# A depthwise convolution and a feed-forward block on one core: the fourth input load in one transfer, the last group but one added on VectorE, and the order of work in the first groups

## The chip, the core and the metric

The kernel runs on one core of a Trainium2 chip. The core has five engines that run side by side, each with its own queue of instructions: TensorE (PE, matmuls; its weight loads are listed as PEld), VectorE (DVE), ScalarE (ACT), GpSimd (POOL) and SyncE (SP), which here only issues transfers. Transfers (DMAs) run on 16 DMA engines and can be issued from several queues. Time is device microseconds (us) of one launch; lower is better. All times of instructions and transfers below are counted from the start of the span of the profiled execution.

## What is computed

The input x has 8 batches of 4224 positions and 192 channels. A causal convolution of 7 taps runs along the positions; the 192 channels are 8 heads of 24, and all channels of a head share the 7 weights, which are a softmax over the taps. On its result a feed-forward block with a normalisation in front and a residual is applied, with 768 hidden units.

```python
# convolution: w is a softmax over K=7 taps for each of H=8 heads
x_pad = np.concatenate([np.zeros((B, K - 1, D)), x], axis=1)
x_unf = x_pad[:, idx, :].reshape(B, S, K, H, group)
y = np.einsum('hk,bskhg->bshg', w, x_unf).reshape(B, S, D)
# feed-forward block
mu, var = mean and variance of y over D
xn = (y - mu) / np.sqrt(var + 1e-06) * g_ln
out = y + np.maximum(xn @ w_ch1, 0.0) @ w_ch2
```

All of it is float32. The first six positions of every batch see zeros on their left: this is the pad.

## The kernel before

**Groups.** The 33,792 positions are cut into 18 groups (lines 70 to 74). A position lies on one of 128 partitions, and a group holds up to 16 positions of each partition. Group 0 is the first 6 of batch 0, group 1 the 8 positions a partition that are left over from all batches (`LEFT`), group 2 the second 16 of batch 0; then come batches 1 to 7 in two groups each (3 to 16); group 17 is the 10 positions of batch 0 that group 0 left out. Groups 0 and 1 share their buffers (y, yt, ot).

**What a group goes through.** `load_x` brings x of the group, with 6 positions to the left, into a buffer `xg` (two buffers take turns; x3 takes the one of x1, so its load waits until the taps of group 1 are done). Tap products: `first_tap` (line 366) writes tap 0 to `y` on ACT at line 375, `second_tap` (385) and for group 2 `third_tap` write taps 1 and 2 to other buffers at line 383, and `add_in_parts` (402) adds these to y or to one another by four adding transfers that POOL issues at line 406. The other taps are added by `conv` (408) on DVE at line 414. `transpose` (425) makes yt, DVE's `moments` (445) and POOL's `root` (447) make the reciprocal root of the variance, `rstd`. The mean and g_ln are folded into w_ch1, so rstd is needed only at the very end. The up-projection fills sets of four PSUM banks, two sets in turn, and ACT evicts them with the ReLU. The down-projection follows, and `out = y + rstd * ot` ends the group.

**Groups 0 and 1** use a plain form: `up` (541), one chunk of 128 hidden units (f = 0 to 5) after the other, eviction on ACT at line 510, then `down` (809, matmuls at line 807). Between the chunks other ACT work is put by hand. For group 0 that is the tap products of group 1, w1's last copies (`copies_of_w1`, line 357) and `scale_power` (243), a part of decoding the weights. For group 1 it is `between` (534): the tap products of group 3, beginning behind chunk 2's eviction.

**Groups 2 to 17** use a form with seven products in place of eight, in `up_mixed` (600) or, for the last group, `up_last` (728), and in `down_fast` (841). It needs sums and differences of quarters of y and of the weights: `sums_of_y` (582), `sums_of_quarters` (569). Products are closed by DVE at line 640 or 750, or by adding transfers at line 598. A product's matmuls are at line 520 (up) and 860 (down).

**How a group ends.** For all groups but the last, y is stored to `out` by `store_y` (483) from SP. Later ACT scales ot by rstd (`scale`, 943) and POOL issues transfers that add ot to `out` in memory (`add_to_out`, 954). For group 16 this later work stands in `up_last`, except that DVE scales the first four positions (768). The last group adds on DVE (`add`, 956) and stores from SP (`store`, 963).

**The order** of all instructions of an engine is the order in which the program writes them (`manual_schedule`): each engine works through its own queue and stands until what an instruction needs is there. In the pass of the main loop for group 0 (1031 to 1056) stand: `conv` of group 1 in parts, the tap products of group 2, `store_y(1)` (eight stores), `load_x(3)`, moments, `down(0)`, the first part of `root(0)`, the adds of group 2's third tap (1053), the rest of `root(0)` and a difference of w1's quarters.

**The load of x3** is the one that the change touches. With `apart`, `load_x` clears the pad (one partition, 6 positions; line 163, on POOL) and then issues three transfers: partitions 16 to 127, 1 to 15, and partition 0 without the pad. The loads of other first halves of a batch (line 155) are one transfer, with the pad cleared behind it (161).

**The start.** Before w1 is decoded, `keep_warm` (359) issues matmuls whose result nobody reads. One `keep_warm` unit shows as two matmul records of line 362.

Of the kernel before, what the change touches and what calls it, by code (L numbers as in the profile page):

```python
# [11 lines left out]
ALU = mybir.AluOpType  # L12
# [4 lines left out]
def kernel(  # L17
# [29 lines left out]
    nc = tc.nc  # L47
    PSUM = bass.MemoryType.PSUM
    B, S, D = x.shape
    H, K = weight.shape  # L50
    F = moe_w_ch1.shape[1]
    P = 128
# [75 lines left out]

    xg = {}

    def load_x(g, queue=nc.sync, apart=False, gate=False):
        b, j0, n = groups[g]
        t = xpool.tile([P, J + PAD, D], F32, tag="xg", name=f"xg{g}")
        xg[g] = t
        flat = t.rearrange("p j d -> p (j d)")
        if gate:
            nc.vector.memset(t[0 : 1 if b is not None else P, 0:1, 0:1], 0.0)
        if b is None:
            for b in range(B):
                (queue if b < B // 2 else nc.gpsimd).dma_start(  # L140
                    out=flat[LP * b : LP * b + LP, 0 : (PAD + n) * D],
                    in_=bass.AP(
                        tensor=x.tensor, offset=(b * S + P * R - PAD) * D,
                        ap=[[n * D, LP], [1, (PAD + n) * D]],
                    ),
                )
            return
        if j0:
            queue.dma_start(
                out=flat[:, 0 : (n + PAD) * D], in_=xr[b, :, (j0 - PAD) * D : (j0 + n) * D]  # L150
            )
            return
        if b and not apart:

            queue.dma_start(
                out=flat[:, 0 : (PAD + n) * D],
                in_=bass.AP(
                    tensor=x.tensor, offset=(b * S - PAD) * D, ap=[[R * D, P], [1, (PAD + n) * D]]
                ),
            )  # L160
            nc.gpsimd.memset(t[0:1, 0:PAD, :], 0.0)
            return
        nc.gpsimd.memset(t[0:1, 0:PAD, :], 0.0)
        for p0, p1 in ((16, P), (1, 16)):
            nc.sync.dma_start(
                out=flat[p0:p1, 0 : (PAD + n) * D],
                in_=bass.AP(
                    tensor=x.tensor, offset=(b * S + p0 * R - PAD) * D,
                    ap=[[R * D, p1 - p0], [1, (PAD + n) * D]],
                ),  # L170
            )
        nc.sync.dma_start(out=flat[0:1, PAD * D : (PAD + n) * D], in_=xr[b, 0:1, 0 : n * D])
# [69 lines left out]
    def scale_power(power):  # L242
        nc.scalar.activation(power, power, AF.Relu, scale=float(1 << 23), bias=low)
# [297 lines left out]
    def up(g):  # L541


        n = groups[g][2]
        hidden_tile(g)
        for f in range(NF):
            banks = take_set()
            rows_of_tiles(banks, yt[g][:, 0:n], w1[:, :, f * P : f * P + P])
            evict_up(g, f, banks[:, :, 0 : n * C])
            if g == 0 and f == 0:  # L550
                first_tap(1, heads=(0, H // 2))
            elif g == 0 and f == 1:
                copies_of_w1(1, [(q, 1) for q in range(NQ)])
                scale_power(words_2[2])
            elif g == 0 and f < 4:
                first_tap(1, heads=(2 * f, 2 * f + 2))
            between(g, f)

    def quarters_of_w1(f0=0, f1=FC):
# [168 lines left out]
    def up_last(g, ahead, pending):  # L728


        n = groups[g][2]
        w = n * T
        hidden_tile(g)
        a = ht[g]
        a11, a12, a21, a22 = quarters_of_y(g)
        s1, s2, s3, s4 = ysums[g]
        b11, b12, b21, b22 = quarters_of_w1()
        t = [w1sums[:, k] for k in range(3)]
        (c11, c12), (c21, c22) = [
            [a[:, h, e].rearrange("p f q j t -> p f q (j t)") for e in range(2)] for h in range(2)  # L740
        ]

        def seen(banks):
            return banks[:, :, 0 : FC * w].rearrange("p q (f w) -> p f q w", w=w)

        def product(to, left, right, first=True, end=True):
            rows_of_tiles(to, left, right, first, end, True)

        def close(c, banks):
            nc.vector.tensor_tensor(c, c, seen(banks), op=ALU.add)  # L750

        Y, X = take_set(), take_set()
        product(X, a11, b11, True, False)
        nc.scalar.copy(c11, seen(X))
        for step in range(2):
            next(pending, None)
        next(ahead)
        product(Y, a12, b21)
        close(c11, Y)
        size, step = groups[g - 1][2], 4  # L760

        def scaled(j):
            scale(g - 1, j, j + 1)
            if (j + 1) % step == 0:
                add_to_out(g - 1, j + 1 - step, j + 1)

        part, factor = ots[g - 1][:, 0:step], rstd[g - 1][:, 0:step]
        nc.vector.tensor_tensor(
            part, part, factor.unsqueeze(2).to_broadcast([P, step, D]), op=ALU.mult
        )  # L770
        add_to_out(g - 1, 0, step)
        product(X, s2, t[0], False, False)
        nc.scalar.copy(c21, seen(X))
        scaled(step), scaled(step + 1)
        product(Y, s3, t[1], True, False)
        nc.scalar.copy(c22, seen(Y))
        nc.scalar.activation(c11, c11, AF.Relu)
        product(X, s1, b12, False, False)
        close(c22, X)
        product(Y, a22, t[2], False)  # L780
        close(c21, Y)
        product(X, s4, b22, False)
        scaled(step + 2), scaled(step + 3)
        nc.scalar.activation(c22, c22, AF.Relu)
        for j in range(HJ, HJ + step):
            scaled(j)
        nc.scalar.activation(c12, seen(X), AF.Relu)
        lower_sum(g, (PAIR, *range(PAIR)))
        kept = xpool.tile([P, J + PAD, D], F32, tag="xg", name=f"kept{g}")
        kept = kept.rearrange("p j d -> p (j d)")[:, 0 : NF * (n - fast[g]) * P]  # L790
        kept = kept.rearrange("p (j e f q h t) -> p j e f q h t", e=2, f=FC, q=NQ, h=2, t=T)
        rows_left[g] = kept.rearrange("p j e f q h t -> p j (e f) (q h t)")

        def keep(h, e, j):
            nc.scalar.activation(
                kept[:, j - fast[g], e, :, :, h], a[:, h, e, :, :, j], AF.Relu
            )

        return [lambda j=j: scaled(j) for j in range(HJ + step, size)] + [
            lambda h=h, e=e, j=j: keep(h, e, j)  # L800
            for h, e in ((0, 0), (0, 1), (1, 1), (1, 0)) for j in range(fast[g], n)
        ]
# [38 lines left out]
    def down_fast(g, work):  # L841
# [34 lines left out]
        if g + 2 < NG:  # L876
# [1 line left out]
                lambda tap=tap, h=h: tap(g + 2, heads=(h, h + 1))  # L878
                for tap in (first_tap, second_tap) for h in range(H)
            ]  # L880
        behind = (3, 2, 2, 3) if g + 1 < NG else (0, 1, 1, 1)
        product(0, a[:, 0, 0], b[0], c11, True, behind[0])
        product(1, a[:, 1, 0], w2sums[:, 2], c22, True, behind[1])
        product(1, a[:, 1, 1], w2sums[:, 3], c21, False, behind[2])
# [12 lines left out]
        for dst, left, right_of, op in (  # L897
            (inner, a[:, 1, 1], a[:, 1, 0], ALU.add),
            (upper, inner, a[:, 0, 0], ALU.add),
            (right, a[:, 0, 1], inner, ALU.subtract),  # L900
        ):
            for f in order:
                nc.vector.tensor_tensor(dst[:, f], left[:, f], right_of[:, f], op=op)  # L903
        for c in range(CH):
            nc.vector.tensor_tensor(
                c11[:, c], c11[:, c], banks[2 * c + 1][:, 0:w].rearrange("p (j t) -> p j t", t=t),
                op=ALU.add,
            )
# [54 lines left out]
    def store(g, j1, j2):  # L963
# [3 lines left out]
            in_=y[g][:, j1:j2].rearrange("p j d -> p (j d)"),  # L967
        )

    idle = take_bank()  # L970
    keep_warm(9)
    g_cols = take_bank()
    for r in range(2):
        nc.tensor.matmul(
            g_cols[:, r : r + 1], g_row[:, P * r : P * r + P], ones[:, 0:1], start=True, stop=True
        )
    keep_warm(14)
    split_words(*words_1[0])
    tap_matrices(PE_HEADS[2], range(3))
    split_words(*words_1[1])  # L980
# [40 lines left out]
    for g in range(NG):  # L1021
# [9 lines left out]
        if g == 0:  # L1031
            early = CH * C // GRP
            join_low(*words_2)
            conv(1, 1, 5, heads=(0, early))
            join_sign(*words_2)
            join_product(w2flat, *words_2)
            conv(1, 5, K, heads=(0, early))
            transpose(1, 0, CH)
            conv(1, heads=(early, H))
            first_tap(2)  # L1040
            second_tap(2)
            let_in(w1sums[:, 1])
            sums_of_quarters(w1sums[:, 1], w12, w22)
            sums_of_quarters(w1sums[:, 0], w11, w1sums[:, 1])
            store_y(1)
            load_x(3, apart=True, gate=True)
            transpose(1, CH, NC)
            moments(0)
            moments(1)
            down(g)  # L1050
            steps = root(0)
            next(steps)
            add_in_parts(2, tb[2], third[2])
            next(steps)
            sums_of_quarters(w1sums[:, 2], w21, w1sums[:, 0])
            continue
        if g == 1:
# [11 lines left out]
            sums_of_quarters(w2sums[:, 1], b22, w2sums[:, 0])  # L1069
            sums_of_quarters(w2sums[:, 3], b21, w2sums[:, 1])  # L1070
            continue
        if g + 2 < NG:
            store_y(g + 1)
        results = down_fast(g, work)
        if last:
# [41 lines left out]
```

## Time and profile before

| | us |
|---|---|
| median of 3 runs | 957.19 (954.85 to 959.95) |
| the profiled execution, its own time | 957.02 |
| its span | 955.3 |
| PE enters group 2 (first matmul of `up_mixed`) | 86.64 |
| one group in the middle, up and down | 27.6 + 27.3 |
| the last group's up-projection begins | 912.5 |
| last matmul ends | 950.7 |

The page gives for each engine its busy time and its share of the span. Further views list who waited for whom, the chain of work that ended last (each step followed back to what released it), the instructions in order of time, and, for stretches of time, each engine's busy time with the count of instructions in brackets, then the clock that PE was granted (1.00 is full speed), the DMA engines' busy share and the rate in GB/s. `L510` is line 510 of the kernel. A row such as `room<-ps` names what is written and what is read. The square brackets at the end of a row hold the time that the engine stood idle before it and what the profile names as having ended that.

At the start, up to 86.6 us, the work is uneven: PE waits for decoded weights and for evictions. From there to the last group the same 55 us repeat. The last group is shorter (10 positions), and two of its rows go through a plain down-projection (line 807, at 946.5).

### The profile page before, as it was taken

How to read it: one execution, taken by the hardware profiler on the slowest of the kernel's cores; microseconds unless marked ns; L12 is line 12 of the kernel's file. 1: busy time of each engine (PE TensorE's matmuls, PEld its weight loads, DVE VectorE, ACT ScalarE, POOL GpSimd, SP SyncE). 2: the span in 40 equal slices, each digit the busy share in tenths (PEclk: the TensorE clock that was granted, in tenths of full speed). 3: DMA queues.
4: the chain of work that ended last, by engine and by line, in shares of the span. 5: the costliest groups of instructions: out<-in, count | busy, mean ns of one | idle time of the engine just before them, and what ended most of it. 6: DMA issues, size and time to landing. Idle time of an engine off the chain costs nothing.

```text
span 955.3 us, 38512 instructions
## 1 busy us (share of the span) xinstructions
PE 942.7 (99%) x17106; PEld 749.6 (78%) x17106; DVE 891.6 (93%) x1477; ACT 720.4 (75%) x1287; POOL 343.7 (36%) x463
## 2 busy tenths in 40 slices
PE   9989999999999999999999999999999999999997
PEld 7979869687786989677686968778696877869686
DVE  8998799999999999999999999999999999997875
ACT  6855778969687796968778795877779596768553
POOL 2095165141533227141443217231451415332140
PEclk9999999999999999999999999999999999999999
DMA  8397897988979797897978988897978889776623
GB/s 209 116 191 180 201 258 137 247 164 186 222 130 278 133 254 149 213 207 136 263 145 238 171 217 166 165 256 138 258 145 238 165 180 204 131 173 118 107 34 80
DMA packets 38348, 171.94 MB, mean 180 GB/s; under 512 B 4517, under 2 KB 5798, under 8 KB 32039
## 3 DMA queue, kind: packets, MB, share of 16 engines
q0 software_dynamic: 31488, 106.87, 60.9%
q1 hardware_dynamic: 6688, 62.61, 18.3%
q8 instruction: 134, 2.20, 0.9%
q14 instruction: 32, 0.26, 0.1%
q10 hardware_dynamic: 6, 0.00, 0.0%
HBM read 38.92 MB, written 50.92 MB: 94 GB/s over the span
## 4 chain that ended last, share of the span: by engine, by line
PE 90%; DMA 3%; DVE 2%; POOL 2%; ACT 1%; issue 1%; SPq 0%; ACTq 0%; DVEq 0%; POOLq 0%
PE ps L860 44%; PE ps L520 41%; PE ps L807 2%; DVE y L414 2%; DMA xg<-in_x_dram 1%; DMA room<-room 1%; PE ps L362 1%; ACT room L634 1%; PE ps L323 1%; POOL room L598 0%; POOL d L457 0%; SPq L486 0%; POOL r L480 0%; POOL d L475 0%; POOL d L476 0%
## 5 line engine op out<-in xcount | busy, mean ns | idle before, releaser
L414 DVE SCALAR_TENSOR_TENSOR y<-xg,taps,y 128x384 f32<-128x384 f32 (+3 forms) x710 | 359.8, 582 | 3.5 <-ACT room L634 2.3
L860 PE MATMUL ps<-room,w2sums 128*32 128x256 f32 (+1 forms) x4464 | 243.5, 376 | 1.1 <-issue 1.1
L520 PE MATMUL ps<-yt,w 32*128 32x256 f32 (+3 forms) x4092 | 228.2, 367 | 3.6 <-ACT room L510 3.5
L634 ACT COPY room<-ps 128x512 f32<-128x512 f32 (+1 forms) x225 | 180.6, 844 | 63.9 <-PE ps L520 62.4
L520 PEld LDWEIGHTS ps<-yt,w 32*128 32x128 f32 x4092 | 204.5, 186 | 22.1 <-issue 7.3
L860 PEld LDWEIGHTS ps<-room,w2sums 128*32 128x32 f32 x4464 | 148.7, 110 | 90.1 <-issue 1.6
L860 PE MATMUL ps<-room,w 128*32 128x256 f32 (+1 forms) x3456 | 190.5, 373 | 0.2 <-DVE room L640 0.2
L903 DVE TENSOR_TENSOR room<-room 128x1024 f32<-128x1024 f32 x135 | 154.6, 1219 | 16.4 <-PE ps L860 9.3
L860 PEld LDWEIGHTS ps<-room,w 128*32 128x32 f32 x3456 | 112.5, 110 | 70.0 <-DVE room L640 5.4
L520 PE MATMUL ps<-ysums,w1sums 32*128 32x256 f32 (+1 forms) x2304 | 132.2, 371 | 0.0
L954 POOL DMA_DIRECT2D out_dram<-ot x70 | 60.1, 977 | 190.8 <-ACT ot L943 181.6
L520 PEld LDWEIGHTS ps<-ysums,w1sums 32*128 32x128 f32 x2304 | 121.3, 185 | 5.3 <-issue 0.2
L943 ACT ACTIVATE ot<-ot,r 128x192 f32<-128x192 f32 x250 | 105.7, 467 | 0.0
L866 ACT COPY cs<-ps 128x256 f32<-128x256 f32 (+1 forms) x192 | 70.6, 369 | 45.4 <-PE ps L860 45.3
L647 ACT ACTIVATE room<-room 128x1024 f32<-128x1024 f32 x90 | 94.8, 1064 | 3.4 <-DMA room<-parts_cs 3.3
L406 POOL DMA_DIRECT2D y<-tb x59 | 52.2, 1342 | 113.3 <-ACT room L866 98.1
L375 ACT ACTIVATE y<-xg,taps 128x384 f32<-128x384 f32 (+3 forms) x141 | 72.9, 610 | 6.2 <-POOL d L476 5.6
L520 PE MATMUL ps<-yt,w1sums 32*128 32x256 f32 (+1 forms) x1152 | 71.8, 371 | 0.7 <-ACT room L634 0.7
L520 PE MATMUL ps<-ysums,w 32*128 32x256 f32 (+1 forms) x1152 | 71.2, 369 | 0.0
L445 DVE BATCH_NORM_STATS2 st<-y 128x6 f32<-128x192 f32 x264 | 70.2, 344 | 0.0
L866 ACT COPY room<-ps 128x256 f32<-128x256 f32 (+1 forms) x96 | 35.7, 372 | 40.4 <-PE ps L860 39.7
L383 ACT ACTIVATE tb<-xg,taps 128x384 f32<-128x384 f32 (+1 forms) x120 | 65.6, 628 | 0.0
(124 smaller groups left out, 959.4 us busy)
## 6 DMA issues: line engine op xcount, KB each, us to landing
xg<-in_x_dram SPq DMA_DIRECT2D x14, 2112.0 KB, 15.9
out_dram<-ot POOLq DMA_DIRECT2D x61, 384.0 KB, 9.6
room<-room POOLq DMA_DIRECT2D x45, 512.0 KB, 5.5
y<-tb POOLq DMA_DIRECT2D x58, 384.0 KB, 8.5
out_dram<-y SPq DMA_DIRECT2D x14, 1536.0 KB, 9.2
room<-parts_cs POOLq DMA_DIRECT2D x30, 512.0 KB, 7.0
room<-parts_tb POOLq DMA_DIRECT2D x15, 1024.0 KB, 7.6
xg<-in_x_dram SPq DMA_DIRECT2D x1, 1848.0 KB
```

The source lines that it names most:

```text
L375: nc.scalar.mul(y[g][:, 0:n, cs], xg[g][:, 0:n, cs], taps[:, h, 0:1])
L383: nc.scalar.mul(dst[:, 0:n, cs], xg[g][:, k : k + n, cs], taps[:, h, k : k + 1])
L414: nc.vector.scalar_tensor_tensor(out=y[g][:, 0:n, cs], in0=t[:, k : k + n, cs], scalar=taps[:, h, k : k + 1], in1=y[g][:, 0:n, cs], op0=AL ...
L445: nc.vector.bn_stats(out=sums[g][:, j, :], in_=y[g][:, j, :])
L520: nc.tensor.matmul(banks[:, q, i * w + j1 * t : i * w + j2 * t], right[rows, c, P * i : P * i + P], left[rows, j1:j2, c, :], start=start, ...
L634: nc.scalar.activation(to, of, AF.Relu) if relu else nc.scalar.copy(to, of)
L647: nc.scalar.activation(c, c, AF.Relu)
L860: nc.tensor.matmul(dst[C * q : C * q + C, 0:w], right[:, f, C * c : C * c + C], left[:, f, q], start=(first and f == PAIR), stop=(f == PAI ...
L866: nc.scalar.copy(to[:, c], dst[:, 0:w].rearrange("p (j t) -> p j t", t=t))
L903: nc.vector.tensor_tensor(dst[:, f], left[:, f], right_of[:, f], op=op)
L943: nc.scalar.mul(ots[g][:, j, :], ots[g][:, j, :], rstd[g][:, j : j + 1])
L954: nc.gpsimd.dma_start(out=rows[:, d0:d1], in_=src[:, d0:d1], accum_op=ALU.add)
```

## The change

Five edits:

1. `load_x(3)` takes the path of the other first halves: one transfer for all 128 partitions. Its pad is not cleared there but by `clear_pad(3)`, which POOL runs behind the first part of `root(0)`.
2. Group 16 is no longer stored early and added in memory. Once its rstd is known, DVE adds ot * rstd to y (`whole_last`), 12 positions in `up_last` and 4 in the last `down_fast`, and SP stores four positions at a time. The ACT scalings, the DVE product and the adding transfers of group 16 go, and so does its `store_y`.
3. The second `keep_warm` has 9 units, not 14.
4. The tap products of group 1 on ACT come in other pieces: two heads behind chunk 0, two behind the w1 copies of chunk 1, four behind chunk 3; `scale_power` moves behind chunk 2. DVE's first taps of group 1 run for two heads at a time.
5. In the last `down_fast` the pieces of ACT work left over are spread as (0, 0, 1, 1).

```diff
+    def clear_pad(g):
+        nc.gpsimd.memset(xg[g][0:1, 0:PAD, :], 0.0)
+
-    def load_x(g, queue=nc.sync, apart=False, gate=False):
+    def load_x(g, queue=nc.sync, later=False, gate=False):
...
-        if b and not apart:
+        if b:
...
-            nc.gpsimd.memset(t[0:1, 0:PAD, :], 0.0)
+            if not later:
+                clear_pad(g)
             return
-        nc.gpsimd.memset(t[0:1, 0:PAD, :], 0.0)
+        clear_pad(g)
...
             if g == 0 and f == 0:
-                first_tap(1, heads=(0, H // 2))
+                first_tap(1, heads=(0, H // 4))
             elif g == 0 and f == 1:
                 copies_of_w1(1, [(q, 1) for q in range(NQ)])
+                first_tap(1, heads=(H // 4, H // 2))
+            elif g == 0 and f == 2:
                 scale_power(words_2[2])
-            elif g == 0 and f < 4:
-                first_tap(1, heads=(2 * f, 2 * f + 2))
+            elif g == 0 and f == 3:
+                first_tap(1, heads=(H // 2, H))
...
         close(c11, Y)
-        size, step = groups[g - 1][2], 4
-
-        def scaled(j):
-            scale(g - 1, j, j + 1)
-            if (j + 1) % step == 0:
-                add_to_out(g - 1, j + 1 - step, j + 1)
-
-        part, factor = ots[g - 1][:, 0:step], rstd[g - 1][:, 0:step]
-        nc.vector.tensor_tensor(
-            part, part, factor.unsqueeze(2).to_broadcast([P, step, D]), op=ALU.mult
-        )
-        add_to_out(g - 1, 0, step)
+        whole_last(g - 1, 0, 3 * HJ // 2)
         product(X, s2, t[0], False, False)
         nc.scalar.copy(c21, seen(X))
-        scaled(step), scaled(step + 1)
...
-        scaled(step + 2), scaled(step + 3)
         nc.scalar.activation(c22, c22, AF.Relu)
-        for j in range(HJ, HJ + step):
-            scaled(j)
...
-        return [lambda j=j: scaled(j) for j in range(HJ + step, size)] + [
+        return [
...
-        behind = (3, 2, 2, 3) if g + 1 < NG else (0, 1, 1, 1)
+        behind = (3, 2, 2, 3) if g + 1 < NG else (0, 0, 1, 1)
...
+        if g + 1 == NG:
+            whole_last(g - 1, 3 * HJ // 2, groups[g - 1][2])
...
+    def whole_last(g, j1, j2):
+
+        for j in range(j1, j2):
+            add(g, j, ots[g][:, j])
+            if j % 4 == 3:
+                store(g, j - 3, j + 1)
...
-    keep_warm(14)
+    keep_warm(9)
...
             join_low(*words_2)
-            conv(1, 1, 5, heads=(0, early))
+            for h in range(0, early, 2):
+                conv(1, 1, 5, heads=(h, h + 2))
...
-            load_x(3, apart=True, gate=True)
+            load_x(3, later=True, gate=True)
...
             next(steps)
+            clear_pad(3)
             add_in_parts(2, tb[2], third[2])
...
-        if g + 2 < NG:
+        if g + 3 < NG:
             store_y(g + 1)
```

## The prediction

> **What bounds the kernel now.** I read four views in this order: busy shares, what TensorE (PE) waited for, the chain that ended last, and order of time around the one wait that stands out.
>
> ```profile
> PE 942.7 (99%) x17106; PEld 749.6 (78%) x17106; DVE 891.6 (93%) x1477; ACT 720.4 (75%) x1287; POOL 343.7 (36%) x463
> PE ps L520 <- ACT room L510: 3.5, 2, 3.2
> 86.71 27.61 PE ps L520 x504
> 114.33 27.33 PE ps L860 x504
> ```
>
> PE is busy 99% of the span, and from 86.7 us the chain is PE almost without a break, 54.9 us a group. So whatever PE gains before group 2 starts should persist to the end, and work taken from other engines later is worth nothing by itself. PE's own waits add up to little: the one large one is 3.2 us, for an eviction by ScalarE (ACT) at L510. The chain (its rows are start, length, what) and the order of time say what that eviction stood behind:
>
> ```profile
> 51.73 12.80 DMA xg<-in_x_dram
> 64.83 0.04 ACT y L375
> 65.35 1.01 ACT room L510
> 66.41 4.50 PE ps L520 x48
> ```
> ```profile
> 58.90 3.63 POOL L406 DMA_DIRECT2D room<-room  x4
> 58.20 1.02 ACT L510 ACTIVATE room<-ps 128x1024 f32<-128x1024 f32 x1 [1.56 <-PE ps L520]
> 64.83 0.61 ACT L375 ACTIVATE y<-xg,taps 128x384 f32<-128x384 f32 x1 [5.61 <-POOL d L476]
> 66.41 4.50 PE L520 MATMUL ps<-yt,w 32*128 32x256 f32 x48 [3.16 <-ACT room L510]
> ```
>
> The first tap of group 3 (L375, called in `between(1, 2)`) is queued on ACT ahead of the eviction of chunk 3. It needs x3, issued at 51.35 and landed at 51.73 + 12.80 = 64.53. (The releaser named, POOL d L476, is a neighbour in POOL's order: x3's pad was cleared at 53.) PE filled both bank sets at 63.25 and stood until 66.41. The next row is the second half of the price:
>
> ```profile
> 66.41:70.90 4.49, 4.49 (x49) 3.57 (x49) 4.49 (x5) 2.87 (x5) 4.17 (x4) 0.63 0.75 143
> ```
>
> After the stand the granted clock is 0.63, so the last chunk takes 4.50 us; the five chunks before it took 13.23 us, 2.65 each. The wait costs 3.16 + 1.85 = 5.0 us.
>
> **The front: ten idle matmuls fewer.** `keep_warm` 14 to 9 drops ten of the second run's 28 records. The first 18 start about 0.21 us apart, the last ten 0.112 us (6 or 7 per us until 11 us, 11 per us in 12 to 13), so what goes is ten fast ones: 1.1 us, not a third of 5.29. L332 then starts near 11.74 instead of 12.86; its w1f is ready at 10.57. PE feeds the ACT copies of w1 (L357), then ACT L231, then VectorE's (DVE) L247 at 26.69: all 1.1 earlier. But L375 of group 1, at 27.22, needs x1, whose last load is issued at 14.2 and takes 12.4 at most: 26.6. From there 0.6 remains.
>
> [...]
>
> **Tap products of group 1 in pieces** (2+2+4 heads, the DVE taps in pairs of heads). No instruction is added. ACT's order on a 0.35 us pitch: two products at 26.65, eviction of f=1, four w1 copies (4 x 0.37), two products from 29.5. DVE has 8 taps x 0.334 = 2.7 us for the first pair, from 27.13 to 29.8, and waits 0.2. `scale_power` (1.33) ends near 32.2, before DVE's 16 taps end at 32.65 (33.31 before). Conv 1 therefore ends 0.65 earlier, 46.85, and x3 is issued at 50.7. PE no longer waits the 0.8 and 0.5 us it lost around 29.5 and 34; its up-projection of group 1 starts at 48.0 (50.02) and would fill both sets at 61.2. Bounds for this part: 0 to 1.1 on the x3 issue.
>
> **x3 in one transfer, pad cleared behind it.** Before: 1848 + 247.5 + 12 KB, 13.2 us from issue to landing, with the four adding transfers of L406 on the same engines from 58.9. The nearest one-piece load of the same size is x4:
>
> ```profile
> xg<-in_x_dram SPq DMA_DIRECT2D x1, 2112.0 KB, 7.9
> 57.00:58.00 1.00, 1.00 (x24) 0.95 (x24) 1.00 (x3) 0.00 (x0) 0.83 (x3) 1.00 0.94 270
> 76.00:77.00 1.00, 1.00 (x8) 1.00 (x8) 1.00 (x1) 1.00 (x4) 0.00 (x0) 1.00 1.06 456
> ```
>
> The last number is GB/s: the split x3 moved 270 with nothing else on the queues, x4 456. x3 can take between 7.9 and 13.2 us (median of all such loads, under other traffic, 15.9). I take 7.9, the row of the same form and an idle queue, because the adds now stand behind the clear on POOL and cannot overlap x3: landing 58.6. [...]
>
> New wait: POOL's memset (L163, 1.05 us) now waits for the landing. On ACT: 58.6 + 1.15, tap 0.6, eviction 1.0: PE's last chunk can start at 61.35 against its own 61.2. The stand shrinks to 0.15, the clock stays up, the chunk takes 2.65, and the down-projection starts at 64.0 instead of 70.84: **6.8 us**.
>
> **What queues behind the waiting memset.** Four add issues (L406), the rest of `root(0)` and one w1 sum: 11.85 us on POOL (58.90 to 70.75), then the four adds to y3. The adds to tb2 begin 59.75 instead of 58.90; the first took until 71.55 at the most (DVE's L1060, their reader, ran at 72.41), 12.65 after the issue began, now 72.4: DVE's chain to yt2 (3.36 + 3.38) is where it was, 79.1. PE now reaches group 2 at 79.8 (86.64): it fits by 0.7. The third sum on POOL (L594) ends about 0.25 after PE wants it. The adds to y3 move from 77.88 to 71.7, ACT's second taps being done at 70.7, and now share the engines with x4's load: 10.8 alone, up to 17 together, so 82.5 to 88.7; I take 87.5. DVE's taps on y3 start there or at 86.5 when its own work ends; before, they started 2.37 after PE entered the group, now some 8. In that group DVE stood idle twice after that:
>
> ```profile
> 106.87 1.23 DVE L836 SCALAR_TENSOR_TENSOR room<-room 128x1024 f32<-128x1024 f32 x1 [2.82 <-ACT room L647]
> 111.85 2.29 DVE L640 TENSOR_TENSOR room<-room,ps 128x2048 f32<-128x2048 f32 x1 [2.17 <-PE ps L520]
> ```
>
> 5.0 us of cover for 5.6 of lateness; L640 has about 0.3 more before PE stands. I charge 0.4. Without that cover it would be 5.6.
>
> **The end.** Out go twelve ACT scalings (0.47), one DVE product (0.95), four adding transfers and y's early store. In come sixteen DVE adds, eight of which take 2.72 us at L958, 0.34 each, and four stores on SP, whose queue is empty there until 950. Twelve adds, 4.1 us, fit DVE's idle 4.58 before L750 at 925.42 (PE-paced) once the 0.95 is gone, with 1.3 to spare; four, 1.4 us, fit the 1.54 idle before L905. PE shows no wait there but gaps called issue (0.74, 0.32, 0.32) that no edit explains. I take 0, bounds -0.5 and +1.
>
> **Sum.** The profiled execution took 957.02 (span 955.3), 0.2 below the median 957.19. 957.02 - 6.85 + 0.25 + 0.4 = 950.8; with the 0.2, **951.0 us**.
>
> **Rivals.**
> 1. x3 stays slow (270 GB/s is the place, not the form), but free of the adds: 2108 KB at 270 GB/s is 8.0, plus 1.0 until it starts and 1 to 2 of stragglers, landing 60.7 to 61.7. PE stands 2.3 to 3.3; the clock may fall (+1.85). 952.8 to 956. For it: the x0 load, also split, moved 240 to 290; against: x4. Chance 0.22.
> 2. The wait moves to DVE: the adds to y3 land at 89 or later behind x4, L640 is 1.5 to 3 late and PE stands there: 952.4 to 954. For it: y3's adds and x4 start together. Chance 0.1.
> 3. Slower: POOL's clear behind x3 is the new gate. It pays only while x3 lands before 63.7; from there PE starts its last chunk later than 66.41. At the 15.9 us median x3 lands at 66.6, PE resumes at 69.4, 3 us late, the clock down longer: 959 to 962. Against: nothing else moves then. Chance 0.08.
> 4. The front edits do nothing (x1 later still): 0.6 less, inside the forecast.
>
> **How the numbers follow.** Forecast 0.6, its own range 949 to 952.4. A measurement here tells about 0.5% (4.8 us) from no change, so faster begins below 952.4: 0.57 from the forecast; same takes what is left of it, rivals 1 and 2 and most of 3: 0.39; slower, 0.04, is the far end of 3. The range 948.5 to 956.0 takes in rivals 1 and 2 and, below, the 0.5 of the end and a front that gains its full 1.1.
>
> **What would show it.** One load of x3 landing 8 us after its issue; PE's wait on L510 under 1 us and clock 1.00 throughout 60 to 72; group 2 entered near 79.8; DVE's wait before L640 in that group gone; SP stores at 920 to 925 with no wait before L750. Wrong if x3 lands after 61, if PE waits for L425 or L640 in group 2, or if the half clock returns.

## The result, and the profile after

The changed kernel takes **951.42 us** (median of 5 runs, 951.29 to 952.28). The kernel before took 958.72 on the same chip (5 runs, 954.85 to 959.95). The ratio is 0.9933, with an interval of 0.9911 to 0.9955: faster by 0.67%. The profiled execution of the changed kernel took 951.49, its span 949.4 us; before these were 957.02 and 955.3. The runs of the changed kernel lie within 1 us of each other, those of the kernel before within 5. The experiments on the tail come back to that scatter; what they explain is a part of it.

Busy shares of the changed kernel, and what PE waited for (us in total, times, longest):

```profile
PE 938.2 (99%) x17096; PEld 747.9 (79%) x17096; DVE 893.0 (94%) x1492; ACT 716.9 (76%) x1275; POOL 343.6 (36%) x459
PE ps L524 <- ACT room L514: 1.3, 1, 1.3
PE ps L353 <- issue: 1.2, 1, 1.2
```

PE is still the bound. Its stand behind an eviction (L510 before, L514 now, since lines have shifted) fell from 3.2 to 1.3 us, and a new gap of 1.2 us stands at the front, with no releaser that the profile can name. The next fence is the chain of waits of the changed kernel, then its order of time around the stand, then one row of its windows (start and end, length, busy time and count of PE, PEld, DVE, ACT and POOL, granted clock, DMA share, GB/s).

```profile
51.60 8.74 DMA xg<-in_x_dram
63.46 2.87 PE ps L524 x48
```
```profile
60.80 1.05 POOL L132 MEMSET xg<- 1x1152 f32 x1 [2.81 <-DMA xg<-in_x_dram]
61.88 0.61 ACT L379 ACTIVATE y<-xg,taps 128x384 f32<-128x384 f32 x1 [3.80 <-POOL xg L132]
63.46 2.87 PE L524 MATMUL ps<-yt,w 32*128 32x256 f32 x48 [1.35 <-ACT room L514]
```
```profile
63.46:66.30 2.84, 2.84 (x49) 2.40 (x49) 2.84 (x6) 2.84 (x5) 2.84 (x3) 1.00 1.06 187
```

x3 is issued at 51.60 and landed 8.74 later, at 60.34, against 64.53 before. POOL starts its memset 0.46 after the landing, the tap on ACT follows the memset at once, and PE goes on at 63.46 instead of 66.41. The clock stays at 1.00, so the chunk that took 4.50 takes 2.87. PE enters group 2 at 82.06 instead of 86.64.

The other difference is at the end. These are PE's rows in order of time over the last fast down-projection, first before, then after:

```profile
933.70 3.70 PE L860 MATMUL ps<-room,w2sums 128*32 128x128 f32 x128 [0.74 <-issue]
937.72 0.31 PE L860 MATMUL ps<-room,w2sums 128*32 128x128 f32 x3 [0.32 <-issue]
941.74 2.71 PE L860 MATMUL ps<-sums,w2sums 128*32 128x128 f32 x91 [0.32 <-issue]
```
```profile
926.33 2.17 PE L851 MATMUL ps<-room,w 128*32 128x128 f32 x72
928.32 4.11 PE L851 MATMUL ps<-room,w2sums 128*32 128x128 f32 x144
932.25 2.15 PE L851 MATMUL ps<-room,w 128*32 128x128 f32 x72
934.21 4.11 PE L851 MATMUL ps<-sums,w2sums 128*32 128x128 f32 x144
```

After the change the rows follow each other without a bracket. From its first matmul to the plain rows behind it, this projection took 930.38 to 946.52 before, 16.14 us, and takes 926.33 to 940.72 now, 14.39.

So the difference of the two profiled executions divides like this, read off at four points of PE's order:

| PE reaches | before | after | gained since the row above |
|---|---|---|---|
| group 2 | 86.64 | 82.06 | 4.58 |
| the last group's up-projection | 912.51 | 908.46 | -0.53 |
| the last fast down-projection | 930.38 | 926.33 | 0.00 |
| its plain rows | 946.52 | 940.72 | 1.75 |

### The profile page after: what moved, and what is told of

It reads as the page before. It is cut to its first block, busy times and chain, and to the rows that moved or that the text cites. A ratio compares the mean times of both kernels' runs of the same rounds, so it can differ in the third digit from the quotient of the medians.

```text
span 949.4 us, 38485 instructions
## 1 busy us (share of the span) xinstructions
PE 938.2 (99%) x17096; PEld 747.9 (79%) x17096; DVE 893.0 (94%) x1492; ACT 716.9 (76%) x1275; POOL 343.6 (36%) x459
## 4 chain that ended last, share of the span: by engine, by line
PE 92%; DMA 2%; DVE 2%; POOL 1%; ACT 1%; issue 1%; SPq 1%; POOLq 0%; ACTq 0%
PE ps L851 45%; PE ps L524 44%; PE ps L798 2%; DMA xg<-in_x_dram 2%; DVE y L418 1%; DMA room<-room 1%; PE ps L327 1%; SPq L490 0%; ACT room L640 0%; PE ps L353 0%; DVE room L646 0%; PE ps L356 0%; POOL room L604 0%; POOL d L461 0%; ACT w L361 0%
## 5 line engine op out<-in xcount | busy, mean ns | idle before, releaser
L640 ACT COPY room<-ps 128x512 f32<-128x512 f32 (+1 forms) x225 | 180.6, 845 | 63.7 <-PE ps L524 62.5
L947 POOL DMA_DIRECT2D out_dram<-ot x66 | 56.5, 981 | 175.9 <-ACT ot L936 174.0
L936 ACT ACTIVATE ot<-ot,r 128x192 f32<-128x192 f32 x238 | 100.9, 469 | 0.0
L524 PE MATMUL ps<-yt,w1sums 32*128 32x256 f32 (+1 forms) x1152 | 71.7, 371 | 0.4 <-ACT room L640 0.4
```

Of the source, the lines that this page charges most:

```text
L524: nc.tensor.matmul(banks[:, q, i * w + j1 * t : i * w + j2 * t], right[rows, c, P * i : P * i + P], left[rows, j1:j2, c, :], start=start, ...
L640: nc.scalar.activation(to, of, AF.Relu) if relu else nc.scalar.copy(to, of)
L936: nc.scalar.mul(ots[g][:, j, :], ots[g][:, j, :], rstd[g][:, j : j + 1])
L947: nc.gpsimd.dma_start(out=rows[:, d0:d1], in_=src[:, d0:d1], accum_op=ALU.add)
```

## The experiments

Each expectation names its own theories. The questions were, in turn: which edit holds the gain; why the tail gained; whether the front edits are worth anything; and what in edit 1 makes x3 early, the form of the transfer, the engines free of adds, or the clear behind it. The kernel before ran along on the chip each time: its medians were 958.48, 957.62 and 957.84 us.

### Edit 1 alone (e1)

```diff
-            load_x(3, apart=True, gate=True)
+            load_x(3, later=True, gate=True)
...
             next(steps)
+            clear_pad(3)
             add_in_parts(2, tb[2], third[2])
```

> Only the load of x3 in one transfer and its pad cleared behind it; all else as before. Theory A (the load was what PE stood for): x3 is issued at 51.3 as before, lands 8 to 9 us later, the clear ends near 61.5, PE's stand of 3.16 us before its last up-chunk of group 1 shrinks below 0.5, the half clock is gone, PE enters group 2 at 81.8 to 82.3 in place of 86.64, and the run is 4 to 5 us shorter than before. Theory B (the gain needs the earlier front too): the stand stays above 1.5 us and the run gains 1 to 3 us.

Measured: 952.63 us (952.51 to 952.86), ratio 0.9934 (0.9920 to 0.9949). x3 was issued at 51.63 and landed at 60.17, PE stood 0.41 us, the clock was full (the next chunk was through 3.00 us after the eviction that let it start, 4.63 before), and group 2 began at 81.89. The tail kept gaps (0.74, 0.32, 0.14) and its 16.14 us. Edit 1 alone gives the whole step into group 2, with nothing of the front edits.

### The front edits alone (e2)

```diff
             if g == 0 and f == 0:
-                first_tap(1, heads=(0, H // 2))
+                first_tap(1, heads=(0, H // 4))
...
-    keep_warm(14)
+    keep_warm(9)
...
-            conv(1, 1, 5, heads=(0, early))
+            for h in range(0, early, 2):
+                conv(1, 1, 5, heads=(h, h + 2))
```

> Only ten idle matmuls fewer and the tap products of group 1 in other pieces. Theory A: worth nothing, since conv of group 1 ends within 0.3 us of 47.5 (PE stands about 1.2 us before the w1 copies at 27 us, and DVE waits for the second pair of products), x3 is issued at 51.3 to 51.7, PE stands about 1.1 us longer before its last up-chunk, and enters group 2 within 0.5 us of 86.64; time within 1 us of before. Theory B (my prediction's): x3 issued 0.65 earlier and the run 0.6 shorter.

Measured: 958.41 (955.33 to 961.12, 10 runs), ratio 0.9997 (0.9981 to 1.0012): nothing. PE's order of time in this kernel:

```profile
27.85 0.93 PE L349 MATMUL ps<-room 32*128 32x384 f32 x8 [2.15 <-issue]
```

The idle matmuls are gone, and 2.15 us of "issue" stand in front of the w1 copies; x3 was issued at 52.11, later than before, and the stand was 4.25 us. The tail of this execution is worth a note too: its three gaps were 0.51, 0.60 and 2.24, and the projection took 19.7 us with the same instructions that took 16.14 in the profile of before. So the tail of before is not one number.

### The tail alone, edits 2 and 5 (e3)

```diff
-        add_to_out(g - 1, 0, step)
+        whole_last(g - 1, 0, 3 * HJ // 2)
...
-        if g + 2 < NG:
+        if g + 3 < NG:
             store_y(g + 1)
```

> Only the end: group 16 added on DVE, stored once, no adding transfers for it. Theory A: PE enters group 2 at 86.6 as before; the gaps of 0.74, 0.32 and 0.32 us that PE had in the last down-projection are gone, first matmul of it to the last of the kernel takes 18.5 us in place of 20.25, and the run is 1.5 to 2 us shorter. Theory B (my prediction's): the gaps stay, time within 0.5 us of before.

Measured: 953.92 (951.89 to 955.32), ratio 0.9946 (0.9925 to 0.9967). Of the profiled executions, this one (955.32) is 1.7 us under that of before. No gap was left in the tail, which ran from 930.73 to 944.79, 14.1 us. Group 2 began at 85.99 behind a stand of 2.07 and the half clock (the next chunk was through 4.68 us after the eviction that let it start).

Edit 1 and the tail's edits each gave more than half of the whole, so they don't add. One reading is worked out from the profiles: e1 still has a tail of 16.14, and the kernel with both (e7, below) one of 13.89. That is 2.25, and the medians of the two are 2.27 apart. Then 2 us is what the tail costs in its short form, and runs of before with a longer one, such as the 19.7 of e2, are what puts its median above its profiled 957.02. The runs that were only timed have no trace, so this is inferred. The tail can't be all of the scatter either: e11 (below) has no adding transfers there and spread over 4.1 us, and e3 over 3.4, both with the split load. The kernels with one transfer and none of these adding transfers (the changed one, e4, e7, e8, e9, e12) spread over 1.0 to 2.5.

### What in the tail: the adding transfers taken out, and put back (e5, e6)

e5 is the kernel before without the adding transfers of group 16; the ACT scalings stay:

```diff
-            if (j + 1) % step == 0:
-                add_to_out(g - 1, j + 1 - step, j + 1)
...
-        add_to_out(g - 1, 0, step)
```

> The kernel before without the adding transfers of group 16 (its feed-forward part is left out of the output; ACT and DVE still scale it, y is still stored early). Theory A (the adding transfers delay PE's next block of instructions): the gaps called issue in the last down-projection are gone, that projection takes 14 to 14.5 us in place of 16.1, and the run is 2 us or more shorter. Theory B (ACT's scalings between the evictions hold PE): the gaps stay, time within 1 us of before.

e6 is the changed kernel with four adding transfers into a buffer that nobody reads, each issued where its source is ready in the last group:

```diff
+    def spare_add(i, src):
+        dst = xg[NG - 1].rearrange("p j d -> p (j d)")[:, 4 * D * i : 4 * D * (i + 1)]
+        nc.gpsimd.dma_start(out=dst, in_=src, accum_op=ALU.add)
...
+        spare_add(0, y[g - 1][:, 0:4].rearrange("p j d -> p (j d)"))
...
+        spare_add(1, hidden(a, 0, 0))
...
+        spare_add(2, hidden(a, 0, 1))
...
+            spare_add(3, y[g - 1][:, 12:16].rearrange("p j d -> p (j d)"))
```

> The changed kernel with four adding transfers of 384 KB put back in the last group, from finished tiles into a dead buffer; no output depends on them. Theory A: PE gets gaps of 0.3 to 2 us each again at blocks of instructions in the last down-projection (1 to 3 us together), time 1 to 3 us over the changed kernel's 951.4. Theory B: no gaps, time within 0.5 us of 951.4.

Measured: e5 954.40 (ratio 0.9967, 0.9954 to 0.9979), e6 954.79 (0.9970, 0.9954 to 0.9987), ten runs each. PE's order of time, first without the transfers (e5), then with idle ones (e6):

```profile
932.03 4.11 PE L857 MATMUL ps<-room,w2sums 128*32 128x128 f32 x144
937.92 4.11 PE L857 MATMUL ps<-sums,w2sums 128*32 128x128 f32 x144
```
```profile
928.78 3.57 PE L854 MATMUL ps<-room,w2sums 128*32 128x128 f32 x122 [0.38 <-issue]
934.17 2.05 PE L854 MATMUL ps<-room,w 128*32 128x128 f32 x66 [1.69 <-issue]
938.19 2.48 PE L854 MATMUL ps<-sums,w2sums 128*32 128x128 f32 x82 [0.32 <-issue]
```

Taking only the transfers out removes the gaps; putting transfers with no reader in brings them back, at a price of 3.4 us against 951.42 (3.0 in the profiles, 17.4 for 14.4). No compute instruction waits for either, so the transfers themselves delay PE. The unit of the delay can be counted. In every profile with adding transfers in the tail (before, e1, e2, e6 and e10), its gaps fall behind the same counts of PE's records (matmuls and weight loads): 33322, 33578, 33834, each 256 after the last. (e1 has none at the second; e1, e6 and e10 have a small fourth, 0.13 or 0.14, 256 further on.) The page of the changed kernel has this row among its DMA queues (packets, MB, share):

```profile
q8 instruction: 134, 2.20, 0.9%
```

134 packets of 2.20 MB are 16 KB each, and the 34,192 matmuls and weight loads of PE, divided by 134, give 255. So PE's instructions appear to come over the DMA engines in blocks of 256, and a block that stands behind other transfers stops PE at its boundary, here for up to 2.24 us. The two kernels show the cause (the transfers), and the traces hold the packets themselves. The 14 profiles have 27 gaps of 0.15 us or more called issue. All 27 stand at such a boundary, and in each PE goes on 1.25 to 1.60 us after an instruction packet has ended; no boundary is passed sooner than about 1.2 us after its packet. Take the packet for the first of the three places: with adding transfers in the tail (five profiles) it starts 2.2 to 2.7 us after PE passed the boundary before, without them (nine) 0.0 to 0.8 us. Earlier groups have adding transfers too and hardly a gap. There PE works on a block for some 6.9 us, and only 3.5 us in the last fast down-projection, so there is more time for a late packet.

### How many idle matmuls, and the front edits undone (e4, e7)

e4 is the changed kernel with `keep_warm(14)` again, e7 the changed kernel with both front edits undone.

```diff
-    keep_warm(9)
+    keep_warm(14)
```

> The changed kernel with the second run of idle matmuls back at 14. Theory A (the idle matmuls are not on the path, and PE pays for their absence at a block of instructions that is not there yet): the 1.2 us gap before the w1 copies at 27 us is gone, x3 is issued within 0.4 us of 51.6, PE enters group 2 within 0.4 us of 82.06, time within 0.6 us of the changed kernel's 951.4. Theory B: the run is about 1 us longer than the changed kernel.

```diff
-    keep_warm(9)
+    keep_warm(14)
...
-                first_tap(1, heads=(0, H // 4))
+                first_tap(1, heads=(0, H // 2))
...
-            for h in range(0, early, 2):
-                conv(1, 1, 5, heads=(h, h + 2))
+            conv(1, 1, 5, heads=(0, early))
```

> The changed kernel with both front edits undone (14 idle matmul units, the tap products of group 1 as before). Theory A (the front edits are worth nothing): x3 is issued within 0.3 us of 51.4, PE enters group 2 at 81.5 to 82.3, time 949.8 to 951, as with 14 units alone (950.1). Theory B (the pieces of tap products help): 0.5 us or more over the 950.1 of the kernel with 14 units and the new pieces.

Measured: e4 950.13 (949.51 to 951.96, ratio 0.9911, 0.9894 to 0.9929), e7 950.36 (949.55 to 951.30, ratio 0.9930, 0.9907 to 0.9952). Both medians are 1.1 to 1.3 us below the changed kernel's, though each has runs that reach into its range, so 14 units are not slower and perhaps 1 us faster than 9. No effect of the pieces of the taps is seen: e4 has them, e7 does not, and they are 0.23 apart. At the place where the changed kernel shows its 1.20 us gap, e4 shows this:

```profile
26.35 0.64 PE L524 MATMUL ps<-yt,w 32*128 32x192 f32 x9 [0.30 <-issue]
```

The gap of the changed kernel stands behind PE record 441, and 441 is 697 less 256, another place where gaps are seen (0.16 at 697 in the kernel before). With 14 units record 441 is another instruction, and 0.30 is left. One profile doesn't settle this: with 9 units the gap at 441 was 2.15 (e2), 1.20 (after), 0.87 (e12), 0.20 (e9) and none in e6 and e11; with 14 it was never over 0.30. In e4 x3 was issued at 51.08, 0.5 earlier, and group 2 began at 81.43. What decides is when the instruction packet comes. For the gap of 1.20 it started at 24.19 and ended at 25.85. In e6, whose front has the same instructions as the changed kernel's, it started at 22.83 and ended at 24.20; there was no gap, group 1's taps ended at 46.41, x3 was issued at 50.27, and group 2 began at 80.67.

### x3 ahead of the stores (e12, e8)

e12 is the changed kernel with the load of x3 issued ahead of the stores of y1 on SP; e8 the same with 14 units.

```diff
-            store_y(1)
             load_x(3, later=True, gate=True)
+            store_y(1)
```

> The changed kernel as it is (9 idle units) with x3's load put ahead of the eight stores of y1. Theory A: PE's stand of 1.35 us is gone, group 2 is entered at 80.6 to 80.9, time 949.8 to 950.4. Theory B: no gain, since PE's first waits (a block of instructions at 27 us) or the stores of y1 take its place; time within 0.4 us of 951.4.

> The changed kernel with 14 idle units and with x3's load put ahead of the eight stores of y1 on SP. Theory A (what is left of PE's stand is x3's place behind 3.6 us of store issues): x3 is issued 3.6 us earlier, near 48, lands near 57, its clear ends by 59.2, PE's stand of 1.2 to 1.35 us is gone, group 2 is entered 1.2 us earlier than with 14 units alone, time 948.5 to 949.3. Theory B: the stores of y1 now land behind x3, and the first tap of group 3, which reuses y1's buffer, waits for them: no gain, or a loss of up to 1 us.

Measured: e12 951.16 (949.87 to 951.69), e8 951.78 (950.36 to 951.90). Neither gains, though in both the stand behind the eviction is gone and group 2 begins earlier, at 81.06 and 80.62 (82.06). PE's order of time in e12, in group 2:

```profile
110.26 1.93 PE L851 MATMUL ps<-room,w 128*32 128x256 f32 x32 [1.52 <-DVE room L646]
```

In the changed kernel PE's waits on DVE's L646 come to 0.2 us in all. Here PE is 1.0 us earlier, DVE is not, and 1.52 is handed back; in e8 PE stands 0.61 and 1.14 us in the same place, for DVE and for an eviction of ACT. With 82 us at the entry to group 2, DVE is only just in time, and an earlier x3 by itself buys nothing. Where DVE's own work was early too, more was kept: e6 entered group 2 at 80.67, and reached the last group's up-projection at 907.33 (908.46 after, 908.55 in e12), although a gap called issue cost it 0.88 on the way.

### The clear behind the adds (e9)

```diff
             next(steps)
-            clear_pad(3)
             add_in_parts(2, tb[2], third[2])
+            clear_pad(3)
             next(steps)
```

> The changed kernel with the clear of x3's pad behind the four adds of group 2's third tap on POOL, so that the adds overlap x3's load as before the change. Theory A (it was the overlap with the adds as much as the form that made x3 late): x3 lands 1 us or more later than 60.3, the clear ends after 62.5, PE's stand is 2.5 us or more and the half clock may return; time 1 to 4 us over 951.4. Theory B (the form alone decides): x3 lands by 60.5, only the clear's place costs: PE stands 2 to 2.6 us, time 0.5 to 1.3 us over 951.4.

Measured: 950.68 (949.83 to 950.84), ratio 0.9924 (0.9906 to 0.9942). The adds were issued from 58.02 on, so they could run beside the last 2 us of the load; x3 still landed at 60.12. So the adds in flight are not what made x3 late in the kernel before, whose load was already slow in the 7 us ahead of them (windows below). The form decides, as theory B has it, but its price for the clear's place did not come: POOL began the clear at 60.48, and PE stood 0.98 us.

### The split load with the adds held back (e10)

The kernel before, its three transfers kept, with a small POOL copy that reads x3 and so holds the adds until it is in:

```diff
             next(steps)
+            nc.gpsimd.tensor_copy(seen_x, xg[3][:, J + PAD - 1, 0:1])
             add_in_parts(2, tb[2], third[2])
```

> The kernel before (x3 in three transfers, pad cleared ahead) with one small POOL copy that reads x3 put ahead of the four adds, so that the adds wait for x3. Theory A (the adds made x3's last packets late): x3 lands at 60.8 to 61.8 instead of 64.5, PE stands under 0.8 us, no half clock, group 2 is entered by 82.5, time 3.5 to 5.5 us under before. Theory B (three transfers are slow by themselves): x3 lands after 62.5 and at least half of the stand is left.

Measured: 967.53 (965.81 to 968.66), ratio 1.0097 (1.0079 to 1.0115). x3 landed at 63.81, with no add beside it, and PE stood 2.47 us: the split form is slow by itself. The clock stayed at 1.00 behind this stand (the next chunk took 2.87), where it fell to half behind the 2.07 us of e3 (4.68, above), so the length of a stand alone does not decide that. The 1% that e10 lost is a lesson of its own. In order of time, POOL, DVE and PE:

```profile
63.94 6.56 POOL L1054 COPY seen_x<-xg 128x1 f32<-128x1 f32 x1 [4.51 <-DMA xg<-in_x_dram]
70.45 3.63 POOL L407 DMA_DIRECT2D room<-room  x4
87.37 3.36 DVE L1062 TENSOR_TENSOR y<-y,room 128x3072 f32<-128x3072 f32 x1 [16.92 <-DMA room<-room]
94.27 1.25 PE L521 MATMUL ps<-yt,w 32*128 32x128 f32 x10 [9.90 <-DVE yt L426]
```

A copy of one element a partition held POOL for 6.56 us, until DVE's taps were through; the adds then shared the engines with x4's load, DVE waited 16.92 us for them, and PE 9.90 for DVE. This is near the forecast's third rival: POOL waiting behind x3 is safe only as long as x3 is early.

### One load in two pieces (e11)

The changed kernel, its x3 loaded as 112 and 16 partitions, pad cleared behind both:

```diff
-            queue.dma_start(
-                out=flat[:, 0 : (PAD + n) * D],
+            for p0, p1 in ((16, P), (0, 16)) if later else ((0, P),):
+                queue.dma_start(
+                    out=flat[p0:p1, 0 : (PAD + n) * D],
...
```

> The changed kernel with x3 in two transfers, 112 and 16 partitions, both with the pad's columns, cleared behind. Theory A (a piece of 112 rows moves at some 270 GB/s, 128 rows at 430): x3 lands 1.5 us or more later than with one transfer, PE stands 2.5 us or more, time 1 us or more over 951.4. Theory B (the pieces share the engines and only issue time is added): x3 lands within 0.7 us of 60.3 and the time is within 0.7 us of 951.4.

Measured: 956.95 (954.49 to 958.59, 10 runs), ratio 0.9988 (0.9975 to 1.0001): 5.5 us of the gain are gone. x3 landed at 63.21. The windows of x3's first 7 us before, after and in e11 differ in the last number, GB/s; then the stand of e11 in order of time, and the window behind it:

```profile
52.00:59.00 7.00, 7.00 (x140) 6.64 (x136) 7.00 (x13) 3.48 (x5) 6.41 (x12) 1.00 1.03 274
```
```profile
52.00:59.00 7.00, 7.00 (x136) 6.65 (x132) 7.00 (x14) 2.95 (x3) 5.48 (x10) 1.00 0.90 324
```
```profile
52.00:59.00 7.00, 7.00 (x136) 6.65 (x132) 7.00 (x13) 2.40 (x3) 5.19 (x10) 1.00 1.04 284
66.32:71.20 4.88, 4.88 (x48) 3.88 (x48) 3.46 (x7) 2.88 (x5) 4.47 (x8) 0.56 1.06 190
```
```profile
66.32 4.97 PE L526 MATMUL ps<-yt,w 32*128 32x256 f32 x48 [4.77 <-ACT room L516]
```

In the 7 us the DMA engines are busier in the split forms (1.03, 1.04) than in the whole one (0.90) and move less. The trace's DMA records say why: x3 comes as one packet of 16,896 bytes for each partition, and that packet takes longer.

| x3 loaded as | kernels | packets | median of one, us | all packets / 16 engines, us |
|---|---|---|---|---|
| one transfer of 128 rows | after, e1, e4, e6, e7, e9 | 128 | 0.629 | 5.7 to 5.9 |
| the same, stores queued behind it | e8, e12 | 128 | 0.629, 0.683 | 6.2, 6.5 |
| 112 rows, then 16 (or 15 and 1) | before, e2, e3, e5, e10, e11 | 127, 128 in e11 | 0.967 to 1.041 | 8.2 to 8.5 |

Eight kernels on one side, six on the other, with adds beside the load or not, and no overlap. In the kernel before, x2 and x4, each one transfer, also have a median of 0.629. The form of the transfer decides; 2.6 us of the landing are in the packets alone (8.4 in e11 against 5.8).

## Why the prediction was right, step by step

The total came out 0.4 from the forecast, but this hides errors of both signs: x3 gave 2.26 less than its term, the end 1.75 more. That the total is so near is luck. The gain by the medians of all runs, 7.3 us, is further from the 6.2 forecast, since the kernel before ran at 958.72 and not at 957.19.

| step | predicted | measured |
|---|---|---|
| x3 issued | 50.7 | 51.60 |
| from issue to landing | 7.9 | 8.74 |
| from landing to the first tap | 1.15 | 1.54 |
| PE's stand | 0.15 | 1.35 |
| down-projection of group 1 begins | 64.0 | 66.26 |
| gained by then (70.84 before) | 6.84 | 4.58 |
| lost behind it | 0.65 | 0.53 |
| gained in the last down-projection | 0 (bound 0.5) | 1.75 |
| span, sum of the three | 6.2 less | 5.8 less |

**What bounds the kernel: right.** The stand and the half clock (0.50 granted in 67 to 69 us before) were the price, though the half clock cost 1.6 and not 1.85: the chunk behind the stand takes 2.80 at full clock (63.46 to 66.26), where the working took 2.65. PE's order kept whatever it won before group 2, but for 0.53 in small waits. e12 and e8, which were earlier still, lost 1.6 and 2.5 us of their gain by the last group, so this holds only while DVE keeps up.

**x3 in one transfer: mechanism right, size 0.84 short.** The choice between x4's 456 GB/s and the 270 of the split was the decision of the whole forecast. The row of the same form was the nearer one, and e11 and e10 show that the form decides. The opposite view, that pieces cost their issue time alone (theory B of e11, x3 within 0.7 us of 60.3), fell with e11's landing at 63.21: a packet of the 112-row piece took some 1.0 us for 0.63. The argument that the adds "cannot overlap x3" was not needed; e9 lets them overlap and lands at 60.12.

**The clear path: 0.4 short.** The memset took its 1.05, but POOL needed 0.46 after the landing to start it, which the working had put at 0.1.

**The front: the step that failed.** "From there 0.6 remains" and "conv 1 ends 0.65 earlier" did not come: group 1's taps ended at 47.73 (47.50 before). e2 shows nothing gained by the two edits together, and e7 that they may lose 1 us. The working followed engine waits alone and counted the time of the idle matmuls as won; PE stood 1.20 us a little later instead, at a boundary of its instruction blocks, and DVE stood for its tap products:

```profile
27.32 0.93 PE L353 MATMUL ps<-room 32*128 32x384 f32 x8 [1.20 <-issue]
30.81 2.73 DVE L418 SCALAR_TENSOR_TENSOR y<-xg,taps,y 128x192 f32<-128x192 f32 x8 [1.41 <-ACT y L379]
```

The second row is DVE's in the changed kernel: 1.41 us, where the working had 0.2. This is rival 4, whose chance was put inside the forecast. e6 shows that the waits themselves were followed rightly. With no gap there, DVE stood only 0.17 before the second pair of taps:

```profile
29.49 2.73 DVE L418 SCALAR_TENSOR_TENSOR y<-xg,taps,y 128x192 f32<-128x192 f32 x8 [0.17 <-ACT y L379]
```

The taps ended at 46.41 (46.85 forecast), the up-projection of group 1 began at 47.56 (48.0) and x3 was issued at 50.27 (50.7). What the working lacked was the arrival of PE's instructions.

**Behind the waiting memset: 0.65 charged, nothing in group 2.** The adds to tb2 landed at 71.97 (72.4 predicted) and DVE read them at 72.09. The adds to y3 were issued at 78.35, not 71.7, because operations of POOL's root stood for 6.04 us (below) and 3.21 us, and landed at 88.57 (87.5). That is late by the forecast's own bounds, and cost nothing, since PE reached group 2 2.3 later than forecast: the lateness came to 4.5 us (taps on y3 6.88 behind PE's entry, 2.37 before), under the 5.0 of cover. Of DVE's wait there, 2.17 before, this is left:

```profile
107.27 2.29 DVE L646 TENSOR_TENSOR room<-room,ps 128x2048 f32<-128x2048 f32 x1 [0.69 <-PE ps L524]
```

**The end: "gaps called issue that no edit explains" was the mis-sized term.** They were the adding transfers' doing (e5, e6), worth 1.75 in the profile and more in e2's, whose tail took 19.7 us. Even so the changed kernel's 14.39 is not the shortest: e4, e5 and e7 have 13.89. What was forecast of DVE held: twelve adds in 4.04 us (4.1), with a wait left before the next instruction that PE paces.

```profile
915.84 4.04 DVE L951 SCALAR_TENSOR_TENSOR y<-ot,r,y 128x192 f32<-128x192 f32 x12
921.37 2.15 DVE L756 TENSOR_TENSOR room<-room,ps 128x1920 f32<-128x1920 f32 x1 [1.49 <-PE ps L524]
```

**The rivals.** The first (x3 stays slow) named the right danger: 60.34 is only 0.4 before its 60.7; its reason, that the place sets the rate and not the form, fell with e11. The second (the wait moves to DVE) did not come here, but it is what e8 and e12 met as soon as x3 was earlier still. The third needs x3 later than 63.7; e10 shows what it is like.

**A better version.** The lowest median is e4's, the changed kernel with 14 idle units: 950.13, 0.9911 (0.9894 to 0.9929) of before against 0.9933 (0.9911 to 0.9955). The intervals overlap, so a gain of about 1 us over the changed kernel is possible but not shown. The medians of e7 and e9 lie between, and e7's ratio to before, 0.9930, is no better than the changed kernel's. The clear behind the adds together with 14 units was not tried.

## What to carry to other kernels

Load a tile with one transfer over all its partitions and mend the odd corner afterwards: with the clear waiting behind it, the split cost 5.5 us here, by its slower packets and not by its count of issues. When PE shows "issue" gaps, count its records between them; gaps that stand a fixed number apart, 256 here, point to its own instruction stream, and the transfers in flight there, worth 3.4 us in e6, are the first thing to move off the engines. And work taken off an engine at the front, like idle matmuls, is a gain only if what follows is not waiting for something else; look at what is next before booking it.

## What was not expected of the hardware

- **Transfers in flight delay PE's instructions.** Gaps of up to 2.24 us in the tail, behind PE record counts that are 256 apart, came with adding transfers there (before, e1, e2, e6, e10); without them (the other nine profiles) no gap there was over 0.10. Each gap ended 1.25 to 1.60 us behind an instruction packet. Gaps of this kind stand elsewhere too: at the front (1.20 after, 2.15 in e2, 0.30 in e4) and in the down-projection of group 2 (0.88 in e6, 0.72 in e9, 0.81 in e11). There the packet was late as well, but the transfers were not varied, so what made it late there is carried over, not shown.
- **A row of the same 16,896 bytes took 0.63 us in a 128-row transfer and about 1.0 in a 112-row one.** Why is open; no record here shows it.
- **POOL stood while DVE worked through its taps.** In the changed kernel, order of time on POOL and DVE:

```profile
64.11 6.04 POOL L461 TENSOR_SCALAR d<-d 128x14 f32<-128x14 f32 x1
52.28 17.80 DVE L418 SCALAR_TENSOR_TENSOR y<-xg,taps,y 128x384 f32<-128x384 f32 x32
```

The first is an operation on 14 numbers a partition (0.21 to 0.45 us elsewhere, but 3.21 once, beside DVE's add at 72.09); it ended with DVE's taps, at 70.1. In e9 it took 8.59 us, and e10's copy 6.56. The other way round, in the kernel before, POOL's sum of 2.98 us at 67.77 came in first, and one tap of DVE took 2.97 instead of 0.60. In the 6.04 us POOL did not get in between some eleven taps in a row, 0.53 apart. It is not always so. Earlier in the same run of taps, from 53.2 to 58.0, nine operations of POOL in close order took 0.43 to 0.56 each. The three long stands above came after POOL had waited or issued transfers. Why they came is open, and no run here varied it by itself.
- **The full clock came at different times:** its first record stands between 5.8 us (e11) and 12.6 us (e10) after the span's start, at 7.3 in e4 and 12.0 in e7, which both have 14 units, and at 6.1 in the changed kernel against 11.7 before. So the number of idle matmuls alone does not fix it, and what they are worth at the front can't be settled with one profile.
